# Ten homes for seven x^T operands, and the last layer's turns behind the first product

## The chip, the cores and the metric

One core of a Trainium2 chip runs the whole program. The metric is the device time of one execution in microseconds (us). Five engines work beside each other, each through its own queue in order: PE (matmul; its weight loads are listed as PEld), DVE (vector), ACT (scalar), POOL (GpSimd) and SP, which here only issues DMAs. They wait for each other through semaphores.

## What is computed

```python
attn_out = _attn_ref(**attn_kwargs)                  # 2 batches, 8 heads, 768 positions
x = attn_out.transpose(0, 2, 1, 3).reshape(B * S, H * D)   # 1536 x 512
# first layer: 8 experts
for e in range(E):
    h = np.maximum(x @ w1[e], 0.0)                   # 512 x 1024
    out += P[:, e:e + 1] * (h @ w2[e])               # P: a gate balanced in 8 rounds
# last layer
a = x @ w_a                                          # 512 x 1536
b = x @ w_b
return (a * b @ w_out)
```

Everything is in 32-bit floats.

## The kernel before

After the attention (some 100 us) the program is one long row of **steps**. Steps 1 to 63 belong to the first layer (2 batches of 768 tokens, 8 experts, 4 pairs of column blocks each, step 0 being interleaved with the attention); 64 to 87 to the last layer, in twelve rounds `q` of two steps: an even step (`part` 0) for `a` and an odd one (`part` 1) for `b`.

A step multiplies a 512 x 256 block of weights with x^T by seven **products** in place of eight. `product(s, j)` (L313) is six matmuls of 384 columns: each operand, weights and x^T alike, is kept as a rounded high part and a low part (three matmuls), over two blocks of 128 rows. The seven operands of x^T, sums of quarters of x, lie with both parts in `flat`, in seven **homes**; the weights' operands lie in `ring0` to `ring2`. Products go to PSUM bank 6 or 7: `BANK = (6, 6, 7, 6, 7, 6, 7)`. So every product waits until the results that lay in its bank have been taken out; `leave(s, j)` (L332) does this, by ACT for j = 0 (L338), by DVE for the others: L342 (j = 2), L344 (3), L346 and L347 (4), L350 (5), L353 (6).

Behind a product stand **second products** (`second`, `second2`; six matmuls of 512 columns from `hid`, the hidden units of the step or round before, to banks 0 to 5). In the last layer three stand in each step, at the products that `AT` names.

What a product gives in the last layer: in even steps ACT keeps it (L534), in odd ones `multiply` takes it times the kept half (DVE L538), ACT rounds it into `hid` (L539) and DVE makes the low part (`lower`, a subtraction, L164).

The order on each engine is the order in which the program is written out: the calls `work()` after every product issue the next pieces that prepare weights (ACT casts, POOL sums, DVE `lower` into `ring`), `flush()` issues what was put off.

**Turns.** When a batch is done, x for the next layer must be transposed: `x2_turn` (L453) puts three 128 x 128 transposes into bank 7 (L458) and ACT copies them out (L462). In the first layer (steps 34 to 37, two in each) and in the last one (rounds 1 to 4, one in each step: eight turns). In the last layer the turn stands behind product 1.

**Renewing the operands.** For the next batch the seven operands are made anew in halves: ACT writes the high half (`x_split`, L285), DVE the low half (`lower`): 14 of each. All go to the same seven homes, each after the product that used it last. `EVEN`, `FRONT` and `BACK` say behind which product each half comes: for batch 1 in steps 31 and 32, for the last layer's batch 0 in 63 and 64, for its batch 1 in 75 and 76.

In these words p(s.j) is product j of step s.

Of the kernel before, what the change touches and what calls it, by code (L numbers as in the profile page):

```python
# [12 lines left out]
FR = mybir.dt.float32r  # L13
# [6 lines left out]
B, H, S, D = 2, 8, 768, 64  # L20
# [16 lines left out]
PAIRS2 = F2 // 256  # L37
# [6 lines left out]
def fused_kernel(  # L44
# [16 lines left out]
    pe, act, dve, pool, sp = nc.tensor, nc.scalar, nc.vector, nc.gpsimd, nc.sync  # L61
# [9 lines left out]
    flat = const.tile([128, 14 * S], FR, name="flat")  # L71
# [200 lines left out]

    def x_part(j, n):
        return flat[:, (2 * j + n) * S:(2 * j + n + 1) * S]

# [6 lines left out]

    def x_split(ops, j, eng, k=slice(2)):
        hi, lo = (x_part(j, n).rearrange("p (k t) -> p k t", k=2)[:, k] for n in range(2))
        act.copy(out=hi, in_=ops[j][:, k])  # L285
        return lambda: lower(ops[j][:, k], hi, lo, eng)
# [26 lines left out]
    def product(s, j):  # L313
        ps = target(s, j)
        w = cell(CELLS * place(s) + ORDER[j])
        for kk in range(2):
            c0, c1 = slice(kk * 128, kk * 128 + 128), slice(256 + kk * 128, 384 + kk * 128)
            t0 = slice(kk * HT, kk * HT + HT)
            mm3(
                ps, w[:, c0], w[:, c1], x_part(j, 0)[:, t0], x_part(j, 1)[:, t0],  # L320
                kk == 0 and j != 1, kk == 1, check=j > 1,
            )
# [49 lines left out]
    def take(pool):  # L372

        if len(ring) == SLOTS:
            ring[1:], hid[:] = [], []
        ring.append(pool.tile([128, CELLS, 512], FR, name=f"ring{len(ring)}"))
        hid.append(pool.tile([128, 2, 2, S], FR, name=f"hid{len(hid)}"))
        if len(ring) == 2:
            pool.tile([128, 504], F32, name="edge_r")

    def warm():
# [8 lines left out]
        for g in WARM:  # L390
# [13 lines left out]
            if g in EARLY:  # L404
                kind, n, k = EARLY[g][0], *map(int, EARLY[g][1:])
                if kind == "s":
                    a, x, y = (t[:, k] for t in todo[n])
                    dve.tensor_tensor(out=a, in0=x, in1=y, op=ALU.subtract)
                else:
                    later.append(x_split(ops, n, pool, slice(k, k + 1)))  # L410
            if d == 6:
# [8 lines left out]
    def rest():  # L420
# [61 lines left out]
        def renew(plan, r):  # L482
            for n in plan[r] if r < len(plan) else ():
                later.append(x_split(ops, n // 2, dve, slice(n % 2, n % 2 + 1)))

# [10 lines left out]
        for s in range(1, STEPS):  # L496
            for j in range(7):
# [6 lines left out]
                if turns and j == 0:  # L504
                    x2_turn(0, 2 * (s - half - 2))
                if s in (half - 1, half, STEPS - 1):
                    renew(FRONT if s == STEPS - 1 else EVEN, 7 * (s == half) + j)
                for t in AFTER.get(j, ()):
# [54 lines left out]
        for q in range(STEPS2 + 1):  # L563
# [3 lines left out]
            for part in range(2):  # L567
                n = STEPS + 2 * q + part
                for j in range(7):
                    if q < STEPS2:  # L570
                        assert place(n) in ready, n
                        product(n, j)
                        leave(n, j, (keep, multiply)[part])
                    if turning and j == 1:
                        x2_turn(1, 2 * (q - 1) + part)
                    if q == 0 and part == 0:
                        renew(FRONT, 7 + j)
# [550 lines left out]
```

## Time and profile before

| | us |
|---|---|
| median of 3 runs | 1412.9 (1412.7 to 1413.11) |
| the profiled execution | 1412.9 |
| its span, first to last instruction | 1410.8 |
| PE busy (its share of the span) | 1392.4 (99%) |
| DVE busy | 980.5 (70%) |
| POOL busy | 601.5 (43%) |
| ACT busy | 578.7 (41%) |

The profiled execution took the time of the median; 2.1 us lie around its span. PE's busy time overlaps from one matmul to the next, so its 99% hides short waits: those are read from the distance of two starts, or from the idle time in brackets behind a row, with the instruction that ended it.

### The profile page before, as it was taken

What the parts mean: (1) busy time and instruction counts of PE and PEld (TensorE: products, weight loads), DVE (VectorE), ACT (ScalarE), POOL (GpSimd) and SP (SyncE); (2) the same over time, 40 slices, a digit from 0 to 9 for tenths busy, and PEclk for the clock granted to TensorE, in tenths of its full rate; (3) what the DMA queues carried; (4) which work ended last, traced back from release to release, by engine and by line L of the source; (5) the groups of instructions that cost most, each with busy time, mean ns of one, the idle gap of its engine ahead of it and who ended that gap; (6) DMA issues with size and microseconds to landing.
All of it is one profiled execution on the core that took longest, in us unless ns stands there. A gap on an engine that the chain in (4) does not pass through costs nothing.

```text
span 1410.8 us, 20274 instructions
## 1 busy us (share of the span) xinstructions
PE 1392.4 (99%) x7219; PEld 1226.1 (87%) x7219; DVE 980.5 (70%) x1932; ACT 578.7 (41%) x1301; POOL 601.5 (43%) x661
## 2 busy tenths in 40 slices
PE   8999999999999999999999999999999999999998
PEld 5568989988998899989899989998999888888997
DVE  7986877667766766685666766675656876776763
ACT  5774344333343334443343333333333534444442
POOL 6894344444444444444343434443434343313430
PEclk8999999999999999999999999999999999999999
DMA  6312333333233333322243323322222121203111
GB/s 189 117 50 71 116 91 112 91 114 110 89 119 105 114 90 112 103 77 84 89 127 105 105 90 112 119 83 73 62 75 60 60 76 60 76 31 104 61 31 47
DMA packets 143950, 127.06 MB, mean 90 GB/s; under 512 B 8096, under 2 KB 114976, under 8 KB 143840
## 3 DMA queue, kind: packets, MB, share of 16 engines
q1 hardware_dynamic: 143408, 125.42, 29.1%
q8 instruction: 58, 0.95, 0.3%
q14 instruction: 52, 0.43, 0.1%
q10 hardware_dynamic: 432, 0.26, 0.1%
HBM read 112.81 MB, written 12.58 MB: 89 GB/s over the span
## 4 chain that ended last, share of the span: by engine, by line
PE 92%; DVE 5%; POOL 1%; ACT 1%; issue 1%; DMA 0%; POOLq 0%; DVEq 0%; ACTq 0%
PE bank L87 88%; PE bank L820 1%; PE bank L894 1%; DVE so L828 1%; POOL a L852 1%; PE bank L875 1%; DVE ring L164 0%; DVE at L881 0%; PE bank L876 0%; DVE flat L164 0%; DMA small<-in_window 0%; PE bank L458 0%; DVE hid L164 0%; ACT hid L539 0%; DVE sm L845 0%
## 5 line engine op out<-in xcount | busy, mean ns | idle before, releaser
L87 PE MATMUL bank<-flat,ring 128*128 128x384 f32 x3696 | 706.7, 337 | 2.6 <-DVE mid L342 1.5
L87 PE MATMUL bank<-ring,hid 128*128 128x512 f32 x2736 | 686.5, 394 | 0.0
L87 PEld LDWEIGHTS bank<-flat,ring 128*128 128x128 f32 x3696 | 651.6, 188 | 38.8 <-ACT acc L462 3.2
L87 PEld LDWEIGHTS bank<-ring,hid 128*128 128x128 f32 x2736 | 506.5, 188 | 93.3 <-DVE hid L164 2.9
L164 POOL TENSOR_TENSOR ring<-raw,ring 128x512 fp32r<-128x512 f32 x150 | 202.5, 1354 | 388.0 <-ACT ring L196 351.0
L326 ACT ACTIVATE hid<-mid 128x384 fp32r<-128x384 f32 x191 | 100.6, 527 | 407.3 <-DVE mid L346 286.9
L183 POOL TENSOR_TENSOR room<-raw 128x256 f32<-128x256 f32 x86 | 90.5, 1052 | 342.5 <-DVE ring L164 279.6
L344 DVE TENSOR_TENSOR mid<-mid,bank 128x384 f32<-128x384 f32 x87 | 48.0, 552 | 189.6 <-PE bank L87 189.5
L327 DVE SCALAR_TENSOR_TENSOR hid<-mid,hid 128x384 fp32r<-128x384 f32 x191 | 125.5, 657 | 53.2 <-ACT hid L326 45.0
L164 DVE TENSOR_TENSOR ring<-raw,ring 128x512 fp32r<-128x512 f32 (+1 forms) x172 | 139.3, 810 | 0.0
L164 DVE TENSOR_TENSOR ring<-room,ring 128x512 fp32r<-128x512 f32 x172 | 111.7, 684 | 0.0
L338 ACT COPY mid<-bank 128x384 f32<-128x384 f32 x87 | 41.8, 480 | 154.5 <-PE bank L87 154.3
L199 POOL TENSOR_TENSOR room<-raw,room 128x256 f32<-128x256 f32 x86 | 85.2, 991 | 6.7
L191 POOL TENSOR_TENSOR room<-room,raw 128x256 f32<-128x256 f32 x86 | 83.8, 975 | 0.0
L186 POOL TENSOR_TENSOR room<-raw 128x256 f32<-128x256 f32 x86 | 67.3, 782 | 11.4 <-DVE ring L164 9.1
L327 DVE SCALAR_TENSOR_TENSOR hid<-bank,hid 128x384 fp32r<-128x384 f32 x64 | 35.4, 553 | 52.6 <-ACT hid L326 52.6
L837 ACT ACTIVATE ex<-so,mx 128x272 f32<-128x272 f32 (+1 forms) x96 | 47.0, 491 | 26.6 <-DVE mx L828 26.3
L353 DVE TENSOR_TENSOR mid<-mid,bank 128x384 f32<-128x384 f32 x88 | 48.2, 547 | 12.2 <-PE bank L87 12.0
L326 ACT ACTIVATE hid<-bank 128x384 fp32r<-128x384 f32 x64 | 31.5, 492 | 57.9 <-PE bank L87 57.6
L350 DVE TENSOR_TENSOR mid<-mid,bank 128x384 f32<-128x384 f32 x87 | 47.6, 547 | 10.4 <-PE bank L87 10.3
L213 ACT CAST ring<-room 128x512 fp32r<-128x512 f32 x86 | 53.6, 623 | 0.3
L207 ACT CAST ring<-room 128x512 fp32r<-128x512 f32 x86 | 53.5, 622 | 0.0
(155 smaller groups left out, 1154.9 us busy)
## 6 DMA issues: line engine op xcount, KB each, us to landing
raw<-in_moe_w SPq DMA_DIRECT2D x256, 256.0 KB, 2.8
raw<-kept SPq DMA_DIRECT2D x66, 256.0 KB, 3.3
kept<-room SPq DMA_DIRECT2D x36, 256.0 KB, 3.0
raw<-in_moe_w_a SPq DMA_DIRECT2D x12, 512.0 KB, 3.8
raw<-in_moe_w_b SPq DMA_DIRECT2D x12, 512.0 KB, 3.6
raw<-in_moe_w_out SPq DMA_DIRECT2D x12, 512.0 KB, 3.6
out_x<-xt SPq DMA_DIRECT2D x11, 256.0 KB, 2.0
qt<-in_q SPq DMA_DIRECT2D x6, 384.0 KB, 3.2
```

The lines of the kernel that those rows point to most:

```text
L87: pe.matmul(out=dst, lhsT=a, rhs=b, start=start and n == 0, stop=stop and n == 2, skip_group_check=not check,)
L164: eng.tensor_tensor(out=lo, in0=src, in1=hi.bitcast(F32), op=ALU.subtract)
L183: pool.tensor_tensor(out=s1, in0=a21, in1=a22, op=ALU.add)
L186: pool.tensor_tensor(out=s3, in0=a11, in1=a21, op=ALU.subtract)
L191: pool.tensor_tensor(out=s2, in0=s1, in1=a11, op=ALU.subtract)
L199: pool.tensor_tensor(out=s4, in0=a12, in1=s2, op=ALU.subtract)
L207: act.copy(out=halves[0][0], in_=halves[0][2])
L213: act.copy(out=halves[1][0], in_=halves[1][2])
L326: act.activation(out=h[:, 0, f, t0], in_=src, func=ACTF.Relu)
L327: later.append(lambda: dve.scalar_tensor_tensor(out=h[:, 1, f, t0], in0=src, scalar=0.0, in1=h[:, 0, f, t0].bitcast(F32), op0=ALU.max, op1 ...
L344: dve.tensor_tensor(out=m[:, 1], in0=m0, in1=ps, op=ALU.add)
L353: dve.tensor_tensor(out=m[:, 1], in0=m[:, 1], in1=ps, op=ALU.subtract)
```

## The change

Three more homes: a tile `more` of 128 x 6·768. `HOMES` gives, for each of the four batches (two in each layer), where each operand lies; three of each batch's seven lie where nothing of the batch before lies. So halves may be made earlier: `AHEAD`, `LAST` and `FIRST` put six of them into the three steps before the last one of a batch, five into the last and three into the first of the next. For the last layer's second batch the first six go to steps 71, 73 and 74 (`AHEAD2`). Each half is the same ACT copy and DVE subtraction as before; there are 14 for each batch, as before. The pause `held` (no new weights started in step 76 before product 5) goes. And in the last layer the turn stands behind product 0 instead of product 1.

```diff
-    def x_part(j, n):
-        return flat[:, (2 * j + n) * S:(2 * j + n + 1) * S]
+    HOMES = (0, 1, 2, 3, 4, 5, 6), (7, 8, 9, 0, 1, 2, 3), (4, 5, 6, 7, 8, 9, 0), (1, 2, 3, 4, 5, 6, 7)
+    def x_part(age, j, n):
+        m = HOMES[age][j]
+        t, m = (flat, m) if m < 7 else (more[0], m - 7)
...
-        EVEN = ((0, 1), (2,), (3,), (4, 5), (6,), (7,), (8,), (9,), (10,), (11,), (12,), (13,))
-        FRONT = ((0, 1), (2, 3), (4,), (5, 6), (7, 8), (9,), (10, 11), (12,), (13,))
-        BACK = ((), (0,), (1,), (2,), (3,), (4,), (5,), (6, 7), (8, 9), (10, 11), (12,), (13,))
...
+        AHEAD = {(-4, 2): (0, 0), (-4, 5): (0, 1), (-3, 2): (1, 0), (-3, 5): (1, 1), (-2, 2): (2, 0), (-2, 5): (2, 1)}
+        LAST = {1: (3, 0), 2: (3, 1), 3: (4, 0), 5: (4, 1), 6: (5, 0)}
+        FIRST = {0: (5, 1), 1: (6, 0), 2: (6, 1)}
+        AHEAD |= {(-1, j): x for j, x in LAST.items()} | {(0, j): x for j, x in FIRST.items()}
+        AHEAD2 = {(3, 1, 3): (0, 0), (3, 1, 5): (0, 1), (4, 1, 4): (2, 0), (5, 0, 0): (1, 0), (5, 0, 1): (1, 1), (5, 0, 5): (2, 1)}
...
-                    if turning and j == 1:
+                    if turning and j == 0:
                         x2_turn(1, 2 * (q - 1) + part)
...
-                    if (q, part) in ((PAIRS2 - 1, 1), (PAIRS2, 0)):
-
-                        held[0] = q == PAIRS2 and j < 5
-                        renew(BACK, 7 * (q == PAIRS2) + j)
+                    renew(3, AHEAD2.get((q, part, j)))
```

**PE at the turn of step 68** (round 2, even). `bank6` and `bank7` are the products' banks, L87 with `flat` or `more` is a product, L87 with `hid` a second product, L458 the turn. Before:

```order
L87 MATMUL bank7_70<-flat_74,ring1_14486 128x384 x6
L87 MATMUL bank6_69<-flat_74,ring2_14492 128x384 x6
L87 MATMUL bank3_66<-ring1_14486,hid1_14493 128x512 x6
L87 MATMUL bank6_69<-flat_74,ring2_14492 128x384 x6
L458 MATMUL bank7_70<-ident_71,xt_73 128x128 x3
L87 MATMUL bank4_67<-ring1_14486,hid1_14493 128x512 x6
L87 MATMUL bank7_70<-flat_74,ring2_14492 128x384 x6
```

Now (the turn's line is L468):

```order
L87 MATMUL bank7_70<-flat_74,ring1_14487 128x384 x6
L87 MATMUL bank6_69<-flat_74,ring2_14493 128x384 x6
L468 MATMUL bank7_70<-ident_71,xt_73 128x128 x3
L87 MATMUL bank3_66<-ring1_14487,hid1_14494 128x512 x6
L87 MATMUL bank6_69<-flat_74,ring2_14493 128x384 x6
L87 MATMUL bank4_67<-ring1_14487,hid1_14494 128x512 x6
L87 MATMUL bank7_70<-flat_74,ring2_14493 128x384 x6
```

The turn went ahead of one second product and of product 1; between it and the last product that wrote bank 7, p(67.6), only p(68.0) is left.

**DVE in steps 73 and 74** (round 4's odd step, from p(73.5) on, and round 5's even one up to product 2; L164 is `lower`, into `hid`, `ring` or, as a half of an operand, `flat`; L473 sums quarters of x). Before:

```order
L164 TENSOR_TENSOR hid0_14487<-extra_83,hid0_14487 128x384
L350 TENSOR_TENSOR mid_81<-mid_81,bank6_69 128x384
L538 TENSOR_TENSOR room_80<-room_80,mid_81 128x384
L164 TENSOR_TENSOR hid0_14487<-room_80,hid0_14487 128x384
L164 TENSOR_TENSOR ring0_75<-room_80,ring0_75 128x2x256 x2
L353 TENSOR_TENSOR mid_81<-mid_81,bank7_70 128x384
L538 TENSOR_TENSOR room_80<-room_80,mid_81 128x384
L164 TENSOR_TENSOR hid0_14487<-room_80,hid0_14487 128x384
L473 TENSOR_TENSOR xt_73<-acc0_79 128x384
L164 TENSOR_TENSOR ring1_14486<-raw2_78,ring1_14486 128x2x256
L342 TENSOR_TENSOR mid_81<-mid_81,bank7_70 128x384
```

Now, from the half that is new there (L358, L361, L548, L483 and L350 are the lines that were L350, L353, L538, L473 and L342):

```order
L164 TENSOR_TENSOR flat_74<-xt_73,flat_74 128x384
L358 TENSOR_TENSOR mid_81<-mid_81,bank6_69 128x384
L548 TENSOR_TENSOR room_80<-room_80,mid_81 128x384
L164 TENSOR_TENSOR hid0_14488<-room_80,hid0_14488 128x384
L164 TENSOR_TENSOR ring0_75<-room_80,ring0_75 128x2x256 x2
L361 TENSOR_TENSOR mid_81<-mid_81,bank7_70 128x384
L548 TENSOR_TENSOR room_80<-room_80,mid_81 128x384
L164 TENSOR_TENSOR flat_74<-acc0_79,flat_74 128x384
L164 TENSOR_TENSOR hid0_14488<-room_80,hid0_14488 128x384
L164 TENSOR_TENSOR flat_74<-acc0_79,flat_74 128x384
L483 TENSOR_TENSOR xt_73<-acc0_79 128x384
L164 TENSOR_TENSOR ring1_14487<-raw2_78,ring1_14487 128x2x256
```

Three halves came in: one ahead of the fetch of p(73.5), two ahead of that of p(74.2), which follows the last row. The end of this list (the hid, two ring rows and the fetch of product 6) stands in the same order at every odd step's end, in both kernels.

**DVE in step 64**, from the fetch of p(63.6) to that of p(64.3). Before:

```order
L353 TENSOR_TENSOR mid_81<-mid_81,bank7_70 128x384
L164 TENSOR_TENSOR flat_74<-xt_73,flat_74 128x384 x2
L444 SCALAR_TENSOR_TENSOR xt_73<-bank3_66,P_72,xt_73 128x512
L164 TENSOR_TENSOR flat_74<-acc0_79,flat_74 128x384
L164 TENSOR_TENSOR ring2_14492<-raw0_76,ring2_14492 128x256
L327 SCALAR_TENSOR_TENSOR hid1_14493<-mid_81,hid1_14493 128x384
L164 TENSOR_TENSOR flat_74<-acc0_79,flat_74 128x384
L342 TENSOR_TENSOR mid_81<-mid_81,bank7_70 128x384
L444 SCALAR_TENSOR_TENSOR xt_73<-bank4_67,P_72,xt_73 128x512
L344 TENSOR_TENSOR mid_81<-mid_81,bank6_69 128x384
```

Now:

```order
L361 TENSOR_TENSOR mid_81<-mid_81,bank7_70 128x384
L164 TENSOR_TENSOR more_14495<-xt_73,more_14495 128x384
L454 SCALAR_TENSOR_TENSOR xt_73<-bank3_66,P_72,xt_73 128x512
L164 TENSOR_TENSOR more_14495<-xt_73,more_14495 128x384
L164 TENSOR_TENSOR ring2_14493<-raw0_76,ring2_14493 128x256
L335 SCALAR_TENSOR_TENSOR hid1_14494<-mid_81,hid1_14494 128x384
L164 TENSOR_TENSOR flat_74<-acc0_79,flat_74 128x384
L350 TENSOR_TENSOR mid_81<-mid_81,bank7_70 128x384
L454 SCALAR_TENSOR_TENSOR xt_73<-bank4_67,P_72,xt_73 128x512
L164 TENSOR_TENSOR flat_74<-acc0_79,flat_74 128x384
L352 TENSOR_TENSOR mid_81<-mid_81,bank6_69 128x384
```

One half fewer ahead of L444 (which waits for PE), the same two between it and the fetch of p(64.2), one more ahead of the fetch of p(64.3).

## Rows read from the trace of the kernel before

**Rows 1.** The page's first line.
```profile
span 1410.8 us, 20274 instructions
```

**Rows 2.** Busy by stretch: length, then PE PEld DVE ACT POOL (count), clock, DMA.
```profile
310.00:410.00 100.00, 100.00 (x500) 89.94 (x499) 66.14 (x119) 38.76 (x79) 42.44 (x38) 1.00 0.34 103
1160.00:1260.00 100.00, 99.12 (x511) 88.00 (x510) 71.00 (x128) 42.15 (x91) 35.13 (x38) 1.00 0.17 53
```

**Rows 3.** Timeline, steps 67 and 68: start, length, instruction, [idle before <- releaser].
```profile
1155.76 0.55 DVE L346 TENSOR_TENSOR mid<-mid,bank 128x384 f32<-128x384 f32 x1 [0.49 <-PE bank L87]
...
1160.09 1.75 PE L87 MATMUL bank<-ring,hid 128*128 128x512 f32 x6
...
1160.50 1.29 DVE L164 TENSOR_TENSOR ring<-room,ring 128x512 fp32r<-128x512 f32 x2
...
1161.67 1.23 PE L87 MATMUL bank<-flat,ring 128*128 128x384 f32 x6
1161.70 0.55 DVE L353 TENSOR_TENSOR mid<-mid,bank 128x384 f32<-128x384 f32 x1
...
1162.73 0.49 PE L458 MATMUL bank<-ident,xt 128*128 128x128 f32 x3
...
1162.98 1.64 PE L87 MATMUL bank<-ring,hid 128*128 128x512 f32 x6
...
1164.72 0.82 PEld L87 LDWEIGHTS bank<-flat,ring 128*128 128x128 f32 x5 [0.54 <-ACT acc L462]
```

**Rows 4.** Timeline, steps 66 and 67: the fetch of p(66.6), and PE behind p(67.0).
```profile
1147.32 0.55 DVE L353 TENSOR_TENSOR mid<-mid,bank 128x384 f32<-128x384 f32 x1 [1.36 <-PE bank L87]
...
1148.16 1.55 PE L87 MATMUL bank<-ring,hid 128*128 128x512 f32 x6
...
1149.56 1.21 PE L87 MATMUL bank<-flat,ring 128*128 128x384 f32 x6
```

**Rows 5.** Timeline, steps 75 and 76: p(75.6), p(76.0) and DVE ahead of them.
```profile
1255.06 1.21 PE L87 MATMUL bank<-flat,ring 128*128 128x384 f32 x6
1255.37 0.55 DVE L164 TENSOR_TENSOR flat<-acc,flat 128x384 fp32r<-128x384 f32 x1
1255.84 0.55 DVE L350 TENSOR_TENSOR mid<-mid,bank 128x384 f32<-128x384 f32 x1
...
1256.53 0.76 PE L87 MATMUL bank<-flat,ring 128*128 128x384 f32 x3 [0.26 <-DVE mid L350]
```

**Rows 6.** Timeline, step 74: DVE up to the fetch of p(74.2), and p(74.4).
```profile
1236.54 1.12 DVE L164 TENSOR_TENSOR hid<-room,hid 128x384 fp32r<-128x384 f32 x1 [0.58 <-ACT hid L539]
...
1239.20 0.54 DVE L342 TENSOR_TENSOR mid<-mid,bank 128x384 f32<-128x384 f32 x1
...
1239.80 1.34 PE L87 MATMUL bank<-flat,ring 128*128 128x384 f32 x6 [0.31 <-DVE mid L342]
```

**Rows 7.** Timeline, step 64: an operand's half, p(64.4) with p(64.5), the fetch of p(64.3).
```profile
1115.43 1.65 DVE L164 TENSOR_TENSOR flat<-acc,flat 128x384 fp32r<-128x384 f32 x1
...
1117.61 2.43 PE L87 MATMUL bank<-flat,ring 128*128 128x384 f32 x12 [0.69 <-DVE mid L342]
1118.13 0.54 DVE L344 TENSOR_TENSOR mid<-mid,bank 128x384 f32<-128x384 f32 x1
```

**Rows 8.** Timeline, step 32: the last operand's half, and p(32.6) in its second block.
```profile
619.19 1.09 DVE L164 TENSOR_TENSOR flat<-xt,flat 128x384 fp32r<-128x384 f32 x1
...
620.33 0.30 PEld L87 LDWEIGHTS bank<-flat,ring 128*128 128x128 f32 x2 [0.46 <-DVE flat L164]
```

**Rows 9.** Timeline, step 34 of the first layer: a turn behind product 0.
```profile
637.54 0.55 DVE L353 TENSOR_TENSOR mid<-mid,bank 128x384 f32<-128x384 f32 x1
...
638.87 0.49 PE L458 MATMUL bank<-ident,acc 128*128 128x128 f32 x3
```

**Rows 10.** Busy by stretch, as in rows 2, at the program's start.
```profile
5.00:10.00 5.00, 1.44 (x10) 1.21 (x11) 3.12 (x15) 0.00 (x0) 1.47 (x3) 0.75 1.03 357
10.00:15.00 5.00, 4.53 (x19) 3.13 (x16) 4.27 (x23) 3.46 (x15) 1.54 (x5) 0.50 0.37 92
```

More of the change, by code (lines that the diff above doesn't have):

```diff
@@ L271, in fused_kernel, with age @@
     flat_acc = acc[0].rearrange("p t d -> p (t d)")
-    def x_part(j, n):
-        return flat[:, (2 * j + n) * S:(2 * j + n + 1) * S]
+    HOMES = (0, 1, 2, 3, 4, 5, 6), (7, 8, 9, 0, 1, 2, 3), (4, 5, 6, 7, 8, 9, 0), (1, 2, 3, 4, 5, 6, 7)
+    more = []
+    def x_part(age, j, n):
+        m = HOMES[age][j]
+        t, m = (flat, m) if m < 7 else (more[0], m - 7)
+        return t[:, (2 * m + n) * S:(2 * m + n + 1) * S]
+    def age(s):
+        return s // (STEPS // B) if s < STEPS else B + (s - STEPS) // (2 * PAIRS2)
     def x_sums(x, space):
@@ L281, in x_sums, with x_split @@
         return todo, [b11, b21, t2, t3, t1, b22, t4]
-    def x_split(ops, j, eng, k=slice(2)):
-        hi, lo = (x_part(j, n).rearrange("p (k t) -> p k t", k=2)[:, k] for n in range(2))
+    def x_split(ops, new, j, eng, k=slice(2)):
+        hi, lo = (x_part(new, j, n).rearrange("p (k t) -> p k t", k=2)[:, k] for n in range(2))
         act.copy(out=hi, in_=ops[j][:, k])
@@ L374, in take @@
         if len(ring) == SLOTS:
-            ring[1:], hid[:] = [], []
+            ring[1:], hid[:], more[:] = [], [], []
         ring.append(pool.tile([128, CELLS, 512], FR, name=f"ring{len(ring)}"))
         hid.append(pool.tile([128, 2, 2, S], FR, name=f"hid{len(hid)}"))
+        if len(hid) == 2:
+            more.append(pool.tile([128, 6 * S], FR, name="more"))
         if len(ring) == 2:
@@ L409, in warm @@
                 else:
-                    later.append(x_split(ops, n, pool, slice(k, k + 1)))
+                    later.append(x_split(ops, 0, n, pool, slice(k, k + 1)))
             if d == 6:
@@ L473, in step_sum, with renew @@
             dve.tensor_tensor(out=a, in0=x, in1=y, op=ALU.subtract)
-        EVEN = ((0, 1), (2,), (3,), (4, 5), (6,), (7,), (8,), (9,), (10,), (11,), (12,), (13,))
-        FRONT = ((0, 1), (2, 3), (4,), (5, 6), (7, 8), (9,), (10, 11), (12,), (13,))
-        BACK = ((), (0,), (1,), (2,), (3,), (4,), (5,), (6, 7), (8, 9), (10, 11), (12,), (13,))
-        def renew(plan, r):
-            for n in plan[r] if r < len(plan) else ():
-                later.append(x_split(ops, n // 2, dve, slice(n % 2, n % 2 + 1)))
+        AHEAD = {(-4, 2): (0, 0), (-4, 5): (0, 1), (-3, 2): (1, 0), (-3, 5): (1, 1), (-2, 2): (2, 0), (-2, 5): (2, 1)}
[3 more added lines that the diff above has]
+        AHEAD2 = {(3, 1, 3): (0, 0), (3, 1, 5): (0, 1), (4, 1, 4): (2, 0), (5, 0, 0): (1, 0), (5, 0, 1): (1, 1), (5, 0, 5): (2, 1)}
+        AHEAD2 |= {(PAIRS2 - 1, 1, j): x for j, x in LAST.items()} | {(PAIRS2, 0, j): x for j, x in FIRST.items()}
+        def renew(new, what):
+            if what:
+                later.append(x_split(ops, new, what[0], dve, slice(what[1], what[1] + 1)))
         GATE = (7, 8, 10, 11, 12, 14, 15, 16, 19, 20, 21, 24, 25, 26, 28, 29, 30, 33, 34, 35, 38, 39, 40, 42, 43, 44, 47, 48)
@@ L505, in rest @@
                     x2_turn(0, 2 * (s - half - 2))
-                if s in (half - 1, half, STEPS - 1):
-                    renew(FRONT if s == STEPS - 1 else EVEN, 7 * (s == half) + j)
+                renew(1, AHEAD.get((s - half, j)))
+                renew(2, AHEAD.get((s - STEPS, j)))
                 for t in AFTER.get(j, ()):
```

4 lines of the change are left out of this document (2 added, 2 removed).

## The prediction

> **What bounds the kernel now.** I read the busy times by stretch first, then the timeline at each place that the diff touches, and last, from the order of both programs, who stands ahead of whom there. In the body PE is never idle: 500 matmuls in 100 us [rows 2], one each 0.20 us, with DVE busy for two thirds. Work that is moved on DVE, ACT or POOL is worth nothing there; only a stretch in which PE waits can give time. Where batches change and in the last layer it does wait, in pieces of 0.2 to 0.9 us: for a fetch that comes late on DVE [rows 5 to 7], for an operand's low half [rows 8], for the turn's copy on ACT [rows 3]. Each piece is small, so what the change can win is a few microseconds of 1410.8 [rows 1]; what it can lose depends on what the moved turn meets.
>
> **The turn, even steps.** Today p(68.0) has ended by 1160.09, where a second product starts; product 1 follows at 1161.67, the turn at 1162.73, and the second product behind it at 1162.98 [rows 3]. The turn writes bank 7, so it must wait until p(67.6) has been fetched from it. That is DVE's L353, which runs from 1161.70 to 1162.25 [rows 3]. Today it is done 0.48 us before the turn. The changed kernel puts the turn where the second product starts, at 1160.09, and PE takes its instructions in order: everything behind it waits too. Why is L353 so late? It is the end of a chain that begins when p(67.4) is done (L346 at 1155.76, after DVE idled 0.49 us for PE): two fetches, a multiplication, ACT's rounding, its low part, the fetch of product 5, again multiplication, rounding and low part, then two `lower` of weights (1160.50) and only then L353 [rows 3]. The order shows nothing of it moved. DVE starts it when PE lets it, so a later PE makes no room either. The handing over from a DVE fetch to PE took 0.14 us at p(76.0) (1255.84 + 0.55 to 1256.53) [rows 5]. So the turn starts at 1162.25 + 0.14 = 1162.39, and PE stands still for **2.30 us**.
>
> What is given back there: the second product behind today's turn takes 1.74 us to the next start (1162.98 to 1164.72), since product 2 waits for the turn's copy, and the one at 1160.09 takes 1.58, where a free one takes 1.40 (1148.16 to 1149.56) [rows 3, 4]. That is 0.34 + 0.18 = 0.52 us, which the longer way from the turn to product 2 saves. Net 2.30 - 0.52 = 1.78 us, in each of four even steps (66, 68, 70, 72; I take the pattern of 68 for all): **+7.1 us**. Bounds for one: 1.6, if the chain starts a little sooner, and 2.4, if nothing is given back.
>
> **The turn, odd steps.** p(66.6) belongs to an even step, where nothing is multiplied: its L353 waits for PE and ends at 1147.87, 0.29 us before p(67.0) is done at 1148.16 [rows 4]. With 0.14 for the handing over the turn just fits. A copy's wait can be saved: between 0 and 0.34 each, nearer to 0, since the row there shows no gap of that size; I take 0.1, four times: **-0.4**.
>
> **Step 71.** Two of the new halves stand in the chain of the fourth even turn. The one behind product 3 falls into DVE's 0.49 us of idling ahead of L346 [rows 3]. The one behind product 5 goes between the last low part of `hid` and L353. A `lower` of that size holds the next instruction up by 0.47 us (1255.37 to 1255.84) [rows 5]. **+0.5**, up to 0.9 if the first doesn't fit.
>
> **Steps 73 to 76.** One half now stands ahead of the fetch of p(73.5), and one no longer stands ahead of that of p(75.5). The latter place shows what it costs: p(76.0) starts 1.47 us after p(75.6), while a free product takes 1.06 (1161.67 to 1162.73) [rows 3], so PE loses 0.41 us to L350 with the half ahead of it [rows 5]. The same loss moves from 76 to 74: **0**, between -0.4 and +0.4. The five halves that leave step 76 were hidden, since no wait for an operand shows there. `held` goes without effect: POOL's and SP's rows are the same ones, and no weights start earlier.
>
> In step 74 two more stand between p(73.6)'s fetch and L342, and PE already waits for L342 at p(74.4) (1239.20 + 0.54 to 1239.80) [rows 6], so every delay of L342 counts in full. A half costs 0.47 when alone [rows 5]. But POOL works beside them there, and the low part of `hid` took 1.12 us in place of 0.55 [rows 5, 6]. DVE idles 0.58 us ahead of it, waiting for ACT [rows 6], where the first half finds room. Bounds 0.5 and 2.2 (twice 1.1); I take one contended half less some of the overlap that goes with the delay, nearer to the lone row: **+0.9**. The Trainium skill, "SBUF — State Buffer", section "Who interferes with whom", says that DVE's second port pair is shared with GpSimd as an exclusive lock; by that rule alone both halves would be held up whole, and the sum would be 1.3 us higher. The trace agrees that there is contention [rows 6], not that every DVE instruction meets it.
>
> **Step 64.** Here the lighter step 63 ought to help, since p(64.4) waits for L342 (0.69 us idle) [rows 7]. It doesn't: L444 ahead of it waits for PE anyway, and between L444 and L342 stand the same instructions as before, both halves among them (one took 1.65 us [rows 7]). The wait stays. A third half comes between L342 and L344, which p(64.5) needs. L344 ended at 1118.67 [rows 7], about when p(64.4) did, so it adds nearly its 0.47: **+0.45**, between 0 and 1.6.
>
> **Step 32.** p(32.6) waited for the last half, made behind product 4 (PEld idle 0.46) [rows 8]. It is now made behind product 2, four rows earlier. **-0.45**. What would be late next is nothing by the rows before it.
>
> **The other halves**, two in each of steps 28 to 30 and 60 to 62: one ACT copy and one `lower` at 0.5 us each, beside a PE that runs through with DVE at 66% [rows 2]. 0, up to +2 over all twelve if some delay a fetch; a gain is excluded, as PE doesn't wait there.
>
> **Sum.** 7.1 - 0.4 + 0.5 + 0 + 0.9 + 0.45 - 0.45 = +8.1 us on the profiled execution's 1412.9, which is also the median: **1421.0 us**. Adding bounds of single terms rather than all at once, this case alone runs from 1417.5 to 1425.
>
> **Rivals.** *The turn isn't held.* In the first layer a turn stands behind product 0 as well, and there L353 ended at 638.09, 0.78 us before it [rows 9]. If the chain in the odd steps ended before 1160.09, 2.2 us sooner, the 7.1 and the 0.5 would fall away and the 0.52 would be gained four times: 1412.9 - 2.1 - 0.4 + 0.9 + 0.45 - 0.45 = 1411.3; with the two halves of step 74 hidden as well, 1410.4, and with the lighter step 63 shortening the wait of step 64 by 1 to 2 us, 1409. This is the faster end. Against it: in the first layer a second product stands between product 6 and the turn and no multiplication precedes, and in the last layer L353 is at 1161.70 in plain sight. 12%.
>
> *Part of it comes back.* The waits that lie behind the turns (p(74.4), p(76.0): 0.3 to 0.5 us each [rows 5, 6]) could vanish because PE arrives later. They hang on chains that PE itself starts, so I give it 15%; 1419.
>
> *The clock falls.* In the first microseconds PE was busy for 1.44 of 5 us, and the granted clock went to 0.75 and then 0.50 in the next five [rows 10], half of 2.4 GHz. The new pauses of 2.3 to 2.8 us would be the longest of the body. If one of them brings 5 to 10 us at half clock, 2.5 to 5 us are added: 1424 to 1426. The Trainium skill, "TensorE: Matmul & The Clock Gate", section "What's actually happening", calls the slow state the default, which activity releases; no row of this last layer shows it. 5%.
>
> **How the numbers follow.** The forecast as summed has 68%, and with the rival of 1419 83% lie between 1417 and 1425, which I give as the range; 1425 takes in most of the clock's case. A measurement can tell about 0.2% here, 2.8 us. Slower than 1415.7: 68 + 15 + 5 = 88%. Of the 12% of the first rival, 1410.1 divides: 5% faster, 7% the same.
>
> **What would show it.** Right: in rounds 1 to 4 PE's turn starts about 2.3 us after product 0 of the even steps, its wait ended by DVE's fetch of product 6 (L361), and the waits for the turn's copy are gone; p(74.4) waits longer, p(76.0) less, p(32.6) not at all; p(64.4) as before. Wrong: a turn directly behind product 0 in even steps, or a clock under 1.00 behind it.

## The result, and the profile after

The changed kernel takes **1424.2 us** (median of 6 runs, 1423.5 to 1425.5), the kernel before 1412.9 us in the same comparison: a ratio of 1.0082 (95% interval 1.0070 to 1.0094). It is slower, as forecast; the forecast was 1421.0 us in a range of 1417 to 1425. The profiled execution of the changed kernel took 1425.5 us, its span is 1423.7 us, 12.9 us more than in [rows 1].

The first view is busy time by stretch, with the same columns as [rows 2]: a stretch of the body, one of the last layer, and the five microseconds behind the even turns of rounds 1 to 4.

```profile
310.00:410.00 100.00, 100.00 (x499) 89.95 (x498) 66.17 (x119) 38.73 (x79) 42.44 (x38) 1.00 0.34 104
1170.00:1270.00 100.00, 93.84 (x473) 84.65 (x473) 66.42 (x120) 37.36 (x81) 32.66 (x34) 0.97 0.16 51
1138.00:1143.00 5.00, 5.00 (x26) 4.47 (x27) 2.38 (x3) 3.23 (x7) 2.73 (x4) 1.00 0.03 8
1164.00:1169.00 5.00, 5.00 (x19) 4.41 (x20) 2.29 (x3) 2.23 (x6) 2.63 (x3) 0.66 0.02 7
1192.00:1197.00 5.00, 5.00 (x18) 4.36 (x17) 1.88 (x2) 2.54 (x6) 2.12 (x3) 0.66 0.07 20
1220.00:1225.00 5.00, 5.00 (x18) 4.31 (x19) 2.21 (x3) 1.82 (x5) 2.90 (x4) 0.67 0.02 5
```

The body is unchanged. In the last layer PE has lost work in two ways. It is busy for 93.8 of 100 us, where [rows 2] had 99.1: it waits. And behind three of the four even turns the granted clock, the column after POOL, is 0.66 on average: PE counts as fully busy there and finishes 18 or 19 matmuls, where behind round 1's turn it finishes 26.

Next the timeline of steps 67 and 68, the place of [rows 3]. The fetch of product 6, L353 there, is L361 in the changed kernel, and the turn's L458 is L468.

```profile
1159.97 1.90 PE L87 MATMUL bank<-flat,ring 128*128 128x384 f32 x10
...
1161.60 0.56 DVE L164 TENSOR_TENSOR hid<-room,hid 128x384 fp32r<-128x384 f32 x1 [0.58 <-ACT hid L549]
...
1162.07 1.29 DVE L164 TENSOR_TENSOR ring<-room,ring 128x512 fp32r<-128x512 f32 x2
...
1163.28 0.55 DVE L361 TENSOR_TENSOR mid<-mid,bank 128x384 f32<-128x384 f32 x1
...
1163.88 0.55 PE L468 MATMUL bank<-ident,xt 128*128 128x128 f32 x3 [2.01 <-DVE mid L361]
...
1164.18 1.99 PE L87 MATMUL bank<-ring,hid 128*128 128x512 f32 x6
...
1165.97 2.12 PE L87 MATMUL bank<-flat,ring 128*128 128x384 f32 x6
```

The chain stands where it stood, and so does its length: from the low part of `hid` over the two ring lowers to L361. The turn starts 0.05 us after L361 ends (1163.28 + 0.55), and PE has stood idle for 2.01 us. In the other even steps this idle time is 1.79 us (round 1), 2.01 (round 3) and 2.55 (round 4). Behind the turn the six 384-wide matmuls of p(68.1) take 2.12 us; in [rows 3] they took 1.23.

Last, from the timeline at the places of [rows 7] and [rows 6]: what PE waits for at p(64.5) and at p(74.4).

```profile
1118.69 0.97 PE L87 MATMUL bank<-more,ring 128*128 128x384 f32 x4 [0.28 <-DVE mid L352]
...
1253.24 0.97 PE L87 MATMUL bank<-more,ring 128*128 128x384 f32 x4 [1.13 <-DVE mid L350]
```

The wait at p(74.4) has grown from 0.31 to 1.13 us, and p(64.5) has a wait that it did not have.

To set the two executions against each other I matched their products one by one, by the start of each, and noted at which product the lag of the changed kernel changes:

| where | forecast, us | measured, us |
|---|---|---|
| four even turns: wait, less what is given back | 4 x 1.78 = +7.1 | 4 x 1.67 = +6.7 (round 1: 2.34 - 0.67) |
| the same turns in rounds 2 to 4, beyond that | 0 | +4.6 (about 1.5 each) |
| four odd turns | -0.4 | 4 x (0.33 - 0.43) = -0.4 |
| step 71's two halves | +0.5 | +1.2 (0.6 at p(72.0), 0.55 in round 4's wait) |
| steps 73 to 76, p(74.0) and p(76.0) | 0 | +0.41 - 0.43 = 0 |
| step 74 | +0.9 | +0.8 |
| step 64 | +0.45 | +0.47 |
| step 32 | -0.45 | -0.5 |
| smaller shifts at the end of odd steps | 0 | +0.2 |
| sum | +8.1 | +13.0 in these two executions, +11.3 between the medians |

The net price of an even turn is taken from round 1, where the granted clock held. One line stands out: what the even turns of rounds 2 to 4 cost beyond their wait. The theory (A in the expectations) is that this is the granted clock, and that it falls because TensorE stood idle ahead of the turn. The rivals are that the halves now made in these rounds cost it (B), that any stop does it (C), that it needs an earlier pause (D), that something other than DVE's chain holds the turn (E), or that it comes with the late turn whatever PE did meanwhile (F).

### The profile page after: what moved, and what is told of

It is laid out like the page before. It is cut to its first block, busy times and chain, and to the rows that moved or that the text cites. A ratio compares the mean times of both kernels' runs of the same rounds, so it can differ in the third digit from the quotient of the medians.

```text
span 1423.7 us, 20269 instructions
## 1 busy us (share of the span) xinstructions
PE 1396.6 (98%) x7219; PEld 1231.4 (86%) x7219; DVE 982.5 (69%) x1932; ACT 578.6 (41%) x1301; POOL 602.7 (42%) x661
## 4 chain that ended last, share of the span: by engine, by line
PE 91%; DVE 6%; POOL 1%; ACT 1%; issue 1%; DMA 0%; POOLq 0%; DVEq 0%; ACTq 0%
PE bank L87 87%; PE bank L827 1%; DVE so L835 1%; POOL a L859 1%; PE bank L901 1%; DVE ring L164 1%; PE bank L882 1%; DVE hid L164 1%; PE bank L468 0%; ACT hid L549 0%; DVE at L888 0%; DMA small<-in_window 0%; DVE flat L164 0%; PE bank L883 0%; DVE sm L852 0%
## 5 line engine op out<-in xcount | busy, mean ns | idle before, releaser
L87 PE MATMUL bank<-ring,hid 128*128 128x512 f32 x2736 | 688.7, 395 | 0.0
L87 PEld LDWEIGHTS bank<-ring,hid 128*128 128x128 f32 x2736 | 508.8, 188 | 92.8 <-DVE hid L164 2.1
L87 PE MATMUL bank<-flat,ring 128*128 128x384 f32 x2832 | 544.7, 338 | 0.7 <-DVE mid L358 0.6
L87 PEld LDWEIGHTS bank<-flat,ring 128*128 128x128 f32 x2832 | 502.2, 188 | 26.0 <-DVE mid L358 1.7
L164 POOL TENSOR_TENSOR ring<-raw,ring 128x512 fp32r<-128x512 f32 x150 | 202.6, 1354 | 389.1 <-ACT ring L196 351.3
L352 DVE TENSOR_TENSOR mid<-mid,bank 128x384 f32<-128x384 f32 x87 | 48.0, 552 | 186.6 <-PE bank L87 186.3
L87 PE MATMUL bank<-more,ring 128*128 128x384 f32 x864 | 166.3, 336 | 2.7 <-DVE mid L350 2.3
L87 PEld LDWEIGHTS bank<-more,ring 128*128 128x128 f32 x864 | 152.2, 188 | 12.2 <-DVE mid L350 3.2
L164 DVE TENSOR_TENSOR ring<-raw,ring 128x512 fp32r<-128x512 f32 (+1 forms) x172 | 139.8, 813 | 0.0
L164 DVE TENSOR_TENSOR ring<-room,ring 128x512 fp32r<-128x512 f32 x172 | 111.7, 685 | 0.0
L350 DVE TENSOR_TENSOR mid<-mid,bank 128x384 f32<-128x384 f32 x87 | 47.7, 549 | 13.4 <-PE bank L87 12.8
L361 DVE TENSOR_TENSOR mid<-mid,bank 128x384 f32<-128x384 f32 x88 | 48.2, 548 | 12.3 <-PE bank L87 12.2
L358 DVE TENSOR_TENSOR mid<-mid,bank 128x384 f32<-128x384 f32 x87 | 47.7, 548 | 11.9 <-PE bank L87 11.6
```

The lines of the kernel that those rows point to most:

```text
L87: pe.matmul(out=dst, lhsT=a, rhs=b, start=start and n == 0, stop=stop and n == 2, skip_group_check=not check,)
L164: eng.tensor_tensor(out=lo, in0=src, in1=hi.bitcast(F32), op=ALU.subtract)
L350: dve.tensor_tensor(out=m0, in0=m0, in1=ps, op=ALU.add)
L352: dve.tensor_tensor(out=m[:, 1], in0=m0, in1=ps, op=ALU.add)
L358: dve.tensor_tensor(out=m0, in0=m0, in1=ps, op=ALU.add)
L361: dve.tensor_tensor(out=m[:, 1], in0=m[:, 1], in1=ps, op=ALU.subtract)
```

## Which part of the change costs the time

**The turn put back.** The changed kernel, homes and halves kept, with the old place for the last layer's turns:

```diff
-                    if turning and j == 0:
+                    if turning and j == 1:
```

> The changed kernel with the last layer's turns at their old place, behind the second product; the ten homes and the halves spread over steps stay. Theory A (the loss is the early even turns: the wait for the fetch operation of the step before, and what the granted clock loses after that wait): what is left is the sum of the small shifts read in the two traces, step 32 -0.48, the third half of step 64 +0.40, step 71 +0.46, p74.0 +0.24, p74.4 +0.93, p76.0 -0.41, together +1.1, so 1414.0 us (1413.5 to 1414.6), and the granted clock of steps 66 to 73 stays 1.00. Theory B (the halves that now share VectorE and ScalarE with the turns' rounds bring the missing 5 us): about 1418 to 1419, with slow stretches still to be seen near 1165, 1193 and 1221 us.

Measured: 1414.4 us (1414.2 to 1415.1; kernel before 1412.5; ratio 1.0013, interval 1.0004 to 1.0023), the span 1412.4 us, 1.7 above that of before. The stretch of 1164 to 1169 us:

```profile
1164.00:1169.00 5.00, 4.90 (x28) 4.46 (x26) 4.47 (x8) 2.20 (x6) 1.72 (x3) 1.00 0.22 65
```

The granted clock is back at 1.00, and 28 matmuls fit where 19 did. Homes and halves cost under 2 us; most of the difference between +1.1 and the measured +1.9 is step 72, where p(72.2) lost 0.47, which the sum did not have. It waits there for the turn's copy (ACT L472), and this turn starts 0.06 us after L361, which has a new half ahead of it.

**The turn alone.** The kernel before, with its turns moved up and nothing else:

```diff
-                    if turning and j == 1:
+                    if turning and j == 0:
```

> The kernel before with nothing but the last layer's turns moved up by one product. Theory A (early even turns wait, and the clock falls after the wait): four even turns wait some 2.3 us each and give 0.5 back, +7.1, odd turns -0.4, and two or three stretches at granted clock 0.50 after a wait cost up to 1.6 us each: 1422.5 us (1420 to 1424.5), with the falls to be seen within 5 us behind an even turn. Theory B (the clock falls only because the halves load the same rounds): 1419.6 us, even turns at +1.8 each and the granted clock at 1.00 in steps 66 to 73.

Measured: 1423.6 us (1421.6 to 1423.6; ratio 1.0072, interval 1.0056 to 1.0089). The same stretch:

```profile
1164.00:1169.00 5.00, 5.00 (x19) 4.34 (x19) 2.27 (x3) 1.91 (x5) 2.61 (x3) 0.66 0.03 10
```

The stretch reads as in the changed kernel, with none of the halves there. Round 1 costs 2.35 - 0.67 us, as in the table, rounds 2 to 4 some 3.2 each. B is out: the turns alone bring the whole of it, the falls of the clock included.

**The odd turns alone.** The kernel before, turned early in odd steps only:

```diff
-                    if turning and j == 1:
+                    if turning and j == 1 - part:
```

> The kernel before with the turn moved up in the odd steps alone; the even steps turn behind the second product as before. Theory A: the odd turns have no wait in either place, the four give 0.1 each: 1412.5 us (1412.2 to 1412.9), no pause over 0.4 us before an odd turn, granted clock 1.00. Theory B (an early turn costs through its ScalarE copy and its bank wherever it stands, some 1.8 a turn): about 1420.

Measured: 1412.4 us against 1412.5 (ratio 0.9999, interval 0.9989 to 1.0008), the span 0.37 us shorter. Each odd turn first costs 0.33 us, its own time, at the product that it was moved ahead of, and gives 0.43 back at the next one, as in the table. An early turn as such costs nothing; only the even ones have something to wait for.

## What the even turn waits for, and what that does to the clock

**More work ahead of the turn.** The changed kernel, with the even turn behind the second product that follows product 0:

```diff
-                    if turning and j == 0:
+                    if turning and part and j == 0:
                         x2_turn(1, 2 * (q - 1) + part)
...
                             second(STEPS - 1, t)
+                    if turning and not part and j == 0:
+                        x2_turn(1, 2 * (q - 1) + part)
```

> The changed kernel with the even steps' turn moved behind the second product that follows the first product, so that 1.4 us more of TensorE's work stands ahead of it; the odd steps' turn stays early. Theory A (the price is the length of the pause, and the clock falls only after the longer ones): the four pauses go from 2.0 to 2.9 us down to 0.6 to 1.5, which gives back 4 x 1.4 = 5.6 us, and the granted clock stays 1.00, which gives back some 4.9 us more: 1413.7 us (1413 to 1416). Theory C (the clock falls after any stop of TensorE in these rounds, whatever its length): 1418.5 us, with stretches at 0.50 still behind the turns.

Measured: 1415.1 us (ratio 1.0018, interval 1.0008 to 1.0027). The timeline at round 2's turn:

```profile
1161.88 0.55 DVE L361 TENSOR_TENSOR mid<-mid,bank 128x384 f32<-128x384 f32 x1
...
1162.48 0.55 PE L468 MATMUL bank<-ident,xt 128*128 128x128 f32 x3 [0.47 <-DVE mid L361]
```

and its busy time by stretch:

```profile
1164.00:1169.00 5.00, 5.00 (x29) 4.74 (x28) 4.19 (x7) 2.21 (x5) 1.44 (x3) 1.00 0.20 61
```

The turn still waits for L361, but for 0.47 us, and the granted clock stays at 1.00. A pause in these rounds does not always bring it down, so C is out.

**A shorter chain.** The changed kernel, with the step of the weights' stream that issues the two ring lowers moved behind product 6's fetch, in the odd steps of rounds 0 to 3:

```diff
-                    work()
+                    late_ring = part == 1 and 0 <= q < 4
+                    if not (late_ring and j == 5):
+                        work()
+                    if late_ring and j == 6:
+                        work()
```

> The changed kernel with the two lowering operations on ring cells that stand ahead of the odd step's fetch and subtract moved behind them on VectorE, in rounds 0 to 3; the turns stay early. Theory A (the turn waits for VectorE's chain, and this chain holds two operations of about 0.6 us that can stand behind it): the pauses shrink by 1.1 to 1.2 us each, to 0.9 to 1.7, 4 x 1.15 = 4.6 us come back, and no stretch at 0.50 stands behind them, another 4.9: 1414.7 us (1413.5 to 1416.5). Rival E (the turn waits for the matmul's bank or for ScalarE rather than for that chain): the pauses stay above 1.8 us and the time at 1423 to 1425.

Measured: 1416.2 us (ratio 1.0023, interval 1.0014 to 1.0033). The timeline at the same turn:

```profile
1160.78 0.55 DVE L361 TENSOR_TENSOR mid<-mid,bank 128x384 f32<-128x384 f32 x1
1161.24 1.29 DVE L164 TENSOR_TENSOR ring<-room,ring 128x512 fp32r<-128x512 f32 x2
1161.38 0.55 PE L468 MATMUL bank<-ident,xt 128*128 128x128 f32 x3 [0.81 <-DVE mid L361]
```

L361 now precedes the lowers, and the turn comes as soon as L361 is done. The idle times are 0.58, 0.81, 0.81 and 1.35 us, and no stretch of lower clock is left. The time is 1.5 us above the middle of the forecast, within its range. One of the nine times, not profiled, is 1417.7 us, 1.5 above the median; whether the clock fell in it is not known. It is DVE's chain that holds the turn, so E is out.

**The wait filled, first try.** Eight transposes of the identity ahead of the even turn, into the turn's own bank:

```diff
             ps = bank[7][:, 0:HT]
+            for t in range(8 if c == 1 and n % 2 == 0 else 0):
+                pe.transpose(out=ps[:, 0:128], in_=ident, identity=ident)
```

> The changed kernel with eight transposes of the identity into the turn's own bank ahead of each even turn of the last layer: they need nothing that is late, take about 8 x 0.18 = 1.5 us of the wait, and the turn overwrites what they leave, so only TensorE's idleness in the wait changes, not the wait. Theory A (what is lost behind the turn is the granted clock, and it falls because TensorE stood idle): the turn starts when it did, the stretches at 0.50 are gone, the time is 1424.2 - 4.9 = 1419.3 us (1418.5 to 1420.3). Rival F (what is lost behind the turn comes with the late turn itself, whatever TensorE did ahead of it): 1424 us, matmuls behind the turn still at the slow pace.

Measured: 1428.4 us (ratio 1.0105, interval 1.0090 to 1.0121), against both expectations. The timeline at the same turn, which is L470 here:

```profile
1163.99 0.55 DVE L361 TENSOR_TENSOR mid<-mid,bank 128x384 f32<-128x384 f32 x1
...
1164.59 1.09 PE L468 MATMUL bank<-ident 128*128 128x128 f32 x8 [2.00 <-DVE mid L361]
...
1165.52 0.49 PE L470 MATMUL bank<-ident,xt 128*128 128x128 f32 x3
```

My expectation was wrong in saying that they need nothing late. The transposes waited for L361 just as the turn did, 2.00 us, and put the turn off by another 0.93 us (1164.59 to 1165.52). Matched with the changed kernel's products, the four rounds lose 0.84 to 0.97 us each, which is nearly all of the 3.5 us between the two profiled executions (1429.0 and 1425.5), and the clock still falls in rounds 2 to 4. That leaves F undecided, but settles another point. These transposes read nothing but the identity, so the wait is for **bank 7**, which L361 empties, and not for the turn's data.

**The wait filled, with another bank.** Seven matmuls of a tile of zeros, added to an accumulating bank, ahead of the even turns of rounds 2 to 4:

```diff
+                    if turning and part == 0 and j == 0 and q > 1:
+                        for _ in range(7):
+                            pe.matmul(out=bank[TURN[5]][:, 0:128], lhsT=zeros[:, 0:128], rhs=ident,
+                                      start=False, stop=False, skip_group_check=True)
                     if turning and j == 0:
```

> The changed kernel with seven 128-wide matmuls of a tile of zeros between the first product and the even turn, in rounds 2 to 4. They add zero to an accumulating bank that nobody reads there and wait for nothing, so they fill TensorE's wait for bank 7 and leave the wait itself as it is (in the run before this one the filling wrote bank 7 itself and had to wait with the turn). Theory A (behind a wait the granted clock falls, because TensorE stood idle in it): the turns still start 2.0 to 2.6 us after the first product's end, but the stretches at 0.50 behind them are gone: 1424.2 - 4.9 = 1419.3 us (1418.5 to 1420.3), granted clock 1.00 in steps 66 to 73. Rival F (what is lost behind the turn comes with the late turn, whatever TensorE did ahead of it): 1424 us, matmuls behind the turn at twice their usual time.

Measured: 1420.9 us (1420.5 to 1421.1; ratio 1.0057, interval 1.0042 to 1.0072). PE's timeline at the same turn; L586 is the added work, whose seven matmuls stand as 14 records:

```profile
1161.55 1.73 PE L586 MATMUL bank<-ident,edge 128*128 128x128 f32 x14
1163.72 0.55 PE L468 MATMUL bank<-ident,xt 128*128 128x128 f32 x3 [0.45 <-DVE mid L361]
1164.03 1.63 PE L87 MATMUL bank<-ring,hid 128*128 128x512 f32 x6
1165.50 1.23 PE L87 MATMUL bank<-flat,ring 128*128 128x384 f32 x6
```

The same kernel, by stretch:

```profile
1164.00:1169.00 5.00, 5.00 (x27) 4.48 (x26) 2.15 (x3) 3.23 (x7) 2.50 (x3) 1.00 0.03 8
```

The turn is as late as before (1163.72 against 1163.88), but the 384-wide product behind it takes 1.23 us in place of 2.12, and the granted clock is 1.00. F is out: with the same wait, useless work in it gives back 3.3 us between the medians and 4.7 between the two profiled executions. The time is 0.6 above the expected range: I had taken 4.9 from the changed kernel's profiled execution, which lies 1.4 us above its own median, off that median. The changed kernel's six times lie in two groups: 1425.3 and 1425.5, with a granted clock of 0.992 over the whole execution, and four from 1423.5 to 1424.2, with 0.994. The profiled one, with three falls, is of the first; that the others had one fall less is likely, and not shown. Matched product by product, the even turns cost some 1.65 net in rounds 1 to 3 here and 2.2 in round 4, whose wait holds a new half. So a turn's net price is the same in round 1 and behind a filled wait, and each fall costs 1.5 us. Without its falls of the clock the changed kernel takes 1420.9 us, and my sum for the case without them was 1421.0.

**One early even turn only**, that of round 2, in the kernel before:

```diff
-                    if turning and j == 1:
+                    if turning and j == (0 if (q, part) == (2, 0) else 1):
```

> The kernel before with one early turn only, the even one of round 2 (step 68); all the others stay at their place. Theory A (one pause of about 2.3 us is enough for the granted clock to fall): this step costs 2.3 of wait, 0.5 given back and some 1.4 of slower matmuls, +3.2 in the trace, 1415.7 us, with about 3 us at granted clock 0.50 near 1165 us. Theory D (the falls need the pauses of the rounds ahead, as round 1's pause had none behind it): +1.8, 1414.3 us, the granted clock at 1.00 throughout steps 66 to 73.

Measured: 1415.8 us (1414.3 to 1416.4; ratio 1.0017, interval 1.0007 to 1.0027). The turn's row in the timeline:

```profile
1162.15 0.70 PE L458 MATMUL bank<-ident,xt 128*128 128x128 f32 x3 [2.05 <-DVE mid L353]
```

The same kernel, by stretch:

```profile
1162.00:1167.00 5.00, 4.85 (x17) 4.20 (x18) 2.37 (x4) 1.61 (x4) 2.90 (x4) 0.66 0.00 1
```

A single pause of 2.05 us is enough; D as the need for earlier pauses is out. But the nine times lie in two groups, four from 1414.3 to 1414.9 and five from 1415.8 to 1416.4, which are the two forecasts, without the fall and with it. The profiled execution belongs to the second; that the clock did not fall in the first group is likely, and not shown.

**A longer pause in round 1.** The changed kernel, with the last low part ahead of L361 made twice in round 1's chain:

```diff
-            later.append(lambda: lower(a, h[:, 0, f, t0], h[:, 1, f, t0], dve))
+            for _ in range(2 if (s, f, t) == (STEPS + 1, 0, 1) else 1):
+                later.append(lambda: lower(a, h[:, 0, f, t0], h[:, 1, f, t0], dve))
```

> The changed kernel with one VectorE operation of round 1's chain (the low part that is made last ahead of the fetch) made twice, so that the pause of round 1, the only one without a fall of the granted clock behind it (1.79 us of idle TensorE against 2.00 to 2.55 in the others), becomes 0.55 us longer. Theory A (the length of the idle time decides): the granted clock falls there too, so 0.55 of longer wait and some 1.4 of slower matmuls: 1424.2 + 2.0 = 1426.1 us (1425.3 to 1426.8). Theory D (round 1 is spared because no pause stands ahead of it, or for another reason of its place): 1424.7 us, granted clock 1.00 from 1136 to 1160 us.

Measured: 1425.9 us in three runs and 1428.5 in one (ratio 1.0099, interval 1.0083 to 1.0114). The turns of rounds 1 and 2 in the timeline:

```profile
1138.49 0.90 PE L468 MATMUL bank<-ident,xt 128*128 128x128 f32 x3 [2.38 <-DVE mid L361]
...
1165.93 0.55 PE L468 MATMUL bank<-ident,xt 128*128 128x128 f32 x3 [2.02 <-DVE mid L361]
```

The stretch that holds round 1's turn, and the five microseconds behind round 2's:

```profile
1138.00:1143.00 5.00, 4.51 (x16) 3.94 (x17) 2.69 (x4) 1.41 (x3) 3.42 (x4) 0.66 0.00 0
...
1166.00:1171.00 5.00, 5.00 (x26) 4.48 (x27) 2.35 (x3) 3.24 (x7) 2.70 (x3) 1.00 0.01 2
```

With 2.38 us of idle time the clock falls in round 1 too, and p(66.1) comes 2.0 us later, as A said. So round 1 was spared for the length of its pause, not for its place. But the same execution holds a pause of 2.02 us in round 2 *without* a fall: 26 matmuls fit behind it, and 1.5 us come back there. Pauses near 2.0 us can go either way. The time of 1428.5 was not profiled and stays open.

## Halves at other places

The small losses at steps 64, 71, 73 and 74 are halves, or sums, queued on DVE ahead of a subtract that frees a bank. The first attempt to move them, with the even turns at their old place and the odd ones early:

```diff
-        AHEAD |= {(-1, j): x for j, x in LAST.items()} | {(0, j): x for j, x in FIRST.items()}
-        AHEAD2 = {(3, 1, 3): (0, 0), (3, 1, 5): (0, 1), (4, 1, 4): (2, 0), (5, 0, 0): (1, 0), (5, 0, 1): (1, 1), (5, 0, 5): (2, 1)}
+        AHEAD |= {(-1, j): x for j, x in LAST.items()}
+        AHEAD |= {(-1, 4): (5, 1), (0, 0): (6, 0), (0, 3): (6, 1)}
+        AHEAD2 = {(3, 0, 4): (0, 0), (3, 0, 6): (0, 1), (4, 0, 4): (1, 0), (4, 0, 6): (2, 0), (5, 0, 5): (1, 1), (5, 0, 6): (2, 1)}
...
-        SUMS = ((3, 3), (3, 5), (4, 2), (4, 3), (4, 4), (5, 1), (5, 2), (5, 3))
+        SUMS = ((3, 3), (3, 5), (4, 2), (4, 3), (4, 4), (5, 3), (5, 4), (5, 5))
...
-                    if turning and j == 0:
+                    if turning and j == 1 - part:
```

> The changed kernel with even turns behind the second product and odd turns early, and with the halves that met a chain on VectorE moved: the sixth half of a batch into the step ahead of it (two instead of three are left to steps 32 and 64), those of rounds 3 to 5 into even steps, and the sums of step 74 two products later. Theory A (each of the small losses of the change, at steps 64, 71, 73 and 74, is a half or a sum queued ahead of a subtract that frees a bank): step 32 -0.45, odd turns -0.4, the waits ahead of p64.4 (0.85) and p74.4 (0.5) go, p76.0 -0.4, together -2.6 against the kernel before, 1409.9 us (1409.5 to 1411.5). Rival G (the halves only meet other chains at their new places): 1412 to 1414 us, the same as before.

Measured: 1412.6 us (ratio 0.9998, interval 0.9989 to 1.0007). G, the rival, was right. p(74.4) came 0.43 us sooner, but the timeline shows at the start of step 73:

```profile
1220.49 0.55 DVE L358 TENSOR_TENSOR mid<-mid,bank 128x384 f32<-128x384 f32 x1
...
1221.09 1.15 PE L87 MATMUL bank<-flat,ring 128*128 128x384 f32 x5 [0.93 <-DVE mid L358]
```

At p(73.0) PE waits 0.93 us for L358, ahead of which the halves of step 72 now stand; p(71.0) loses half a microsecond in the same way.

**Behind the first products of the even steps.** There DVE has nothing to fetch until product 2:

```diff
-        AHEAD2 = {(3, 0, 4): (0, 0), (3, 0, 6): (0, 1), (4, 0, 4): (1, 0), (4, 0, 6): (2, 0), (5, 0, 5): (1, 1), (5, 0, 6): (2, 1)}
+        AHEAD2 = {(3, 0, 0): (0, 0), (3, 0, 1): (0, 1), (4, 0, 0): (1, 0), (5, 0, 0): (2, 0), (5, 0, 1): (1, 1), (5, 0, 5): (2, 1)}
...
-                    if (q, part, j) == (3, 0, 3):
+                    if (q, part, j) == (2, 0, 3):
                         todo, ops = x_sums(x2t[1], flat_0)
```

> As the run with the halves spread, with its own two new losses taken out: the halves of rounds 3 to 5 stand behind the first two products of the even steps (where VectorE has nothing to fetch for some 3 us) in place of behind products 4 and 6, where they stood ahead of the fetch that frees a bank for p71.0 and p73.0 (0.50 and 1.10 us lost there). Theory A: step 32 -0.45, step 64 -0.1, odd turns -0.4, step 74 -0.5, p76.0 -0.4, in all -1.9 against the kernel before: 1410.8 us (1410 to 1412). Rival G (each half moved away from one chain holds up the next): 1412 to 1413 us.

Measured: 1411.5 us (ratio 0.9991, interval 0.9982 to 1.0000). The waits at p(71.0) and p(73.0) are gone. What is left is p(74.4), where two halves stand ahead of L350 (timeline):

```profile
1239.23 0.97 PE L87 MATMUL bank<-more,ring 128*128 128x384 f32 x4 [0.64 <-DVE mid L350]
```

**Those two put later** in step 74:

```diff
-... (5, 0, 0): (2, 0), (5, 0, 1): (1, 1), (5, 0, 5): (2, 1)}
+... (5, 0, 3): (2, 0), (5, 0, 5): (1, 1), (5, 0, 6): (2, 1)}
```

> As the run before it, with the two halves of step 74 that stood behind its first two products put behind products 3 and 5. There TensorE waited 0.80 us for the subtract that frees the bank of p74.4, against 0.48 in the kernel before and nothing in the first run with spread halves. Theory A (these two halves are what holds that subtract up): the wait goes, p74.4 comes some 0.8 us sooner, 1410.7 us (1410.2 to 1411.5). Rival G (the loss moves to p75.0 or p76.0): 1411.5 us, as the run before.

Measured: **1411.2 us** (1410.9 to 1411.5) against 1412.8 for the kernel before: ratio 0.9988, interval 0.9979 to 0.9997. The wait at p(74.4) is gone, and of the 0.79 us that this gives 0.3 is lost again at p(75.0) and p(75.1). It is faster than both kernels, by 1.6 us against the one before. Not all of that is the homes' doing: matched with the kernel before, the odd turns give 0.4 of it, as they did alone and without new homes, and the 0.47 at p(74.4) may come from the sums, which moved too. The losses that are gone at p(32.6), p(64.4) and p(76.0), 0.4 to 0.5 us each with 0.3 lost again at p(65.0), go with halves that are made earlier. So the three extra homes seem to have a use if the halves stand where DVE is free and the even turn stays behind the second product; no run tried the moved sums or these places of the halves with seven homes.

## Why the prediction came out as it did

The direction, the wait for bank 7 and most terms were right. What failed is the price of an even turn, which I took to be its wait and nothing more; step 71 was sized too small as well. A clock under 1.00 behind the turn, which the prediction names as a sign of being wrong, came in rounds 2 to 4.

- **Even turns.** Forecast: the turn starts when the fetch of product 6 frees bank 7, PE idle for 2.30 us, 1.78 net. Measured: the bracket shows 1.79 to 2.01 us in rounds 1 to 3, but it counts from the modelled end of the last matmul. Counted as in the forecast, from where the next instruction could have started, it is 2.17 in rounds 2 and 3 and 1.96 in round 1; some 1.65 net where the clock held. The handing over was shorter than assumed (0.05 us, not 0.14). Step 68 was not the pattern for round 1: there the pause is 0.2 shorter and 0.2 less is given back, since the second product behind p(66.0) was free before (1.39 us to the next start, not 1.58). That the wait is for the bank was shown by the transposes that read nothing but the identity.
- **The clock.** I had this as a rival of its own at 5%, with 5 to 10 us at half clock for *one* of the pauses, and no share of it in the sum. It happened beside the forecast, not in place of it, and after three pauses rather than one, 1.5 us each: 4.6 us in the profiled execution, 3.3 between medians. The rival's time, 1424 to 1426, is where the result lies, which is luck in part: it had one long fall where there were several short ones. The step that failed is the chance: the one row on the clock came from the program's start [rows 10], and I gave it little weight because no row of the last layer showed a fall. But the kernel before had no pause near 2 us there, so its rows could not have shown one.
- **Step 71** was forecast at 0.5 with a bound of 0.9 if the first half doesn't fit beside DVE's idling; it measured 1.2. The half behind product 5 lengthened round 4's wait (2.55 us against 2.01 with the turns alone). The 0.6 at p(72.0) is the half behind product 3: it took 1.18 us there and not 0.55 (DVE L164 at 1211.87), so it did not fit into the idle 0.49, and the fetch that p(72.0) waits for (L358, 0.36 us idle) came late. The half behind product 5 follows only after that fetch, so it can't be the cause.
- **Steps 64, 74, 32 and the odd turns** came within 0.1 us each; p(74.0) and p(76.0) nearly cancel, as forecast.
- **The rivals on the other side**: the turn was held, in every even step, and nothing of it came back at p(74.4), whose wait grew.

The range held the result because its upper end, 1425, which the bounds of the single terms gave, took in most of the clock's case. The chance of that case was wrong, and with it the likeliest time. That the sum without the clock, 1421.0, meets the 1420.9 of the filled waits is luck in part: the even turns came 0.4 us cheaper than forecast, step 71 0.7 dearer.

## What to carry to other kernels

An instruction that is moved up an in-order engine's queue waits for the last of its needs, and the bank or buffer that it writes counts among these as much as the data that it reads: find the instruction that frees it, and see when it ends. Where a change makes TensorE pause, price the pause twice, once for its length and once for the matmuls behind it at the lower clock, and ask whether useful or useless work could stand in it. Work that has slack on average still has to be placed: put it where its engine has no fetch to make that frees a bank.

## What the runs showed of the hardware

In the profiled executions idle times of TensorE from 0.40 to 1.79 us ahead of an even turn left the granted clock at 1.00. Behind the four idle times of 2.38 to 2.55 us it fell to 0.50. Behind the ten of 2.00 to 2.05 us it fell in nine cases and did not in one, and the two groups of times with a single pause of 2.05 us fit this; what decides these cases was not found. Ahead of each of these waits TensorE had been busy for some 20 us or more without such a pause, at 1.00. A fall lasted 3 to 4 us at half of the full 2.4 GHz and cost about 1.5 us. The Trainium skill, "TensorE: Matmul & The Clock Gate", section "HAM oscillation — how this bites in real kernels", describes a loop in which each wait for data brings the clock down, so that the next tile starts slowly; the traces agree in kind. The waits of that loop are some 3 to 5 us; here the shorter ones above were enough.

A busy column does not show it: in the five microseconds behind such a turn PE is busy for 5.00 of 5.00 us, at 18 matmuls or at 27.
